# Turning the decayed RWKV-7 state with four full-array transposes instead of sixteen identity products, under a refitted schedule planner

## The chip, the cores and the metric

The kernel runs on one core of a Trainium2 chip. A core has five engines with queues of their own: PE (TensorE, the matrix products; PEld is its weight load), DVE (VectorE), ACT (ScalarE), POOL (GpSimd) and SP (SyncE, which here issues all transfers). They meet only through semaphores. The metric is the device time of one execution in microseconds. The kernel before took 717.02 us, the median of three runs (716.88 to 718.17).

## The reference, cut to what matters

```python
# attention block: B, H, S, D = 4, 8, 768, 40; float32
state = zeros(B, H, D, D)
for t in range(S):
    y[:, :, t] = einsum('bhd,bhde->bhe', r[t], state)
    Sa = einsum('bhde,bhe->bhd', state, a[t])
    state = state * w[t][:, :, None, :] - einsum('bhd,bhe->bhde', Sa, b[t])
    state = state + einsum('bhd,bhe->bhde', v[t], k[t])
# dense block on x = y as (3072 tokens, 320)
h = x @ w_in            # 320 -> 2048
g = h * sigmoid(1.702 * h)
out = g @ w_out         # 2048 -> 320
```

Everything is float32. The recurrence runs over 768 tokens for 32 pairs of batch and head, and its output feeds two dense layers.

## The kernel before

**Tiling.** The sequence is cut into 12 chunks of 64 tokens, and each chunk into two *units* (two batches each), 24 units in all: unit i is chunk i // 2, half i % 2. Within a unit the recurrence becomes products of 64x64 blocks. A 128-partition tile is used as two halves of 64, so that four 64x64 products run in the four quarters of the PE array; `mm` (L330) issues all products. The letters e, f, b, u are the bits that name a head, a batch and a half; `slot(b, u, f)` gives a block's place.

**One unit.** `decay` takes logarithms and cumulated sums of w and their exponentials (`FT`, `GT`, `G`, and `wch`, `wz` for the decay over a chunk). `prep` scales a, b and k with them and forms the score blocks `A` and `RV`. `inverse` inverts a triangular block by five doubling steps (`ps_level`), with DVE transposes and copies between them, then `ps_Q` and `ps_T`, which complete the inverse `T`. `solve` reads the old state, forms `B`, multiplies with the inverse (`ps_X`, masked into `M`), and `ps_y` gives both the unit's output and the new state `zraw`. `read_out` and `decayed` make `x`, which goes to DRAM (`x_dram`) and comes back in the order that the dense layers need (`xT_all`); both transfers are SP's.

**The state.** For each unit but the first two, the state `zraw` of unit i - 2 is decayed by `wz` on DVE, into columns 64 to 103 of the eight 104-column blocks of `zr` (L866). `state_turned` transposes it: 16 products with an identity, each a 64x64 block of which 40 columns are wanted, into both banks of a PSUM pair (`ps_zT`). A copy (L878) brings the result to `zT`, `read_state` multiplies r with it (`ps_rz`), and a copy (L889) puts that into columns 0 to 63 of `zr`. The products for `B` and the sums after `ps_y` then read `zr` whole. Each `zr` buffer is cleared once at the start (L440), since products read 64 columns at a stride of 104.

**Dense layers.** `mlp(c)` holds 160 products of 256 columns (`ps_up`) and 128 of 320 columns (`ps_down`) for each chunk. It can start when x of both units of the chunk is back from DRAM and the weights are there. The weights come in eight pieces that are put together on the chip: a transfer, a step on ACT (L478), three on DVE (L482, L486, L490), and an integer addition on POOL (L494, the "join").

**The order.** Nothing is issued as it is written. `plan.add` books a task with a rank, the engines that may run it with an estimated duration on each, and what it reads and writes. `Plan.order` then plays all engines against a clock and lets the free engine take the able task of lowest rank; so it picks the engine too, where several are named. Its constants say what an instruction fetch, a transfer, a semaphore and a slow PE clock cost. `refined` then tries random changes of the ranks of tasks that start in the first 140 us, keeps those with an earlier planned end, and the tasks are issued in the order that results. A changed constant or seed can thus change each engine's order from the first instruction on. PSUM is four pairs of banks, given out by the planner; queues of each engine are in order.

Of the kernel before, what the change touches and what calls it, by code (L numbers as in the profile page):

```python
# [18 lines left out]
FP32 = mybir.dt.float32  # L19
# [4 lines left out]
ACT = mybir.ActivationFunctionType  # L24
# [35 lines left out]
class Plan:  # L60
# [3 lines left out]


    OPENING = 140000.0
    BLOCK, FETCH, AHEAD = 256, 3528.0, 300.0
    BESIDE, LARGE, BESIDE_LARGE = 0.35, 1e6, 0.63
    COLD, WINDOW, SHARE = 2.0, 2600.0, 0.45
    SWITCH = 1290.0  # L70
    MARGIN, STEADY = 0, 1e12
    DELAY = {"PE": 300.0, "DVE": 60.0, "ACT": 60.0, "POOL": 150.0, "SP": 800.0}

    BEGIN = {"PE": 0.0, "ACT": 3300.0, "DVE": 5500.0, "POOL": 10000.0, "SP": 800.0}
    LATENCY, RATE, SPREAD = 2010.0, 417.0, 1.3

    def __init__(self, slots, pairs):
        self.slots, self.pairs = slots, pairs
# [201 lines left out]
def rwkv7_gelu_quick(ctx: ExitStack, tc: tile.TileContext, time_d, v_d, w_d, wc_d, ak_d, b_d, rv_d, w_in, w_out, out):  # L280
    nc = tc.nc
    H, D, S = 8, 40, out.shape[0] // 4
    DM = H * D
# [10 lines left out]
    EARLY = 4  # L294
    BY_PE = 4
    PLAIN = 4
    ROUNDS, WINDOW, SHARE = 4, 5000.0, 1.0
    TRIES, SEED = 300, 1
    RANKS = [14, 16, 20, 24, 35, 37, 39, 41]
    HALF = [slice(0, 64), slice(64, 128)]  # L300
    BITS = (0, 1)
    QUARTERS = [(0, 0), (1, 1), (0, 1), (1, 0)]
# [3 lines left out]
    work = ctx.enter_context(tc.tile_pool(name="work", bufs=1))  # L306
    dram = ctx.enter_context(tc.tile_pool(name="dram", bufs=1, space=bass.MemoryType.DRAM))
    banks = ctx.enter_context(tc.tile_pool(name="banks", bufs=1, space=bass.MemoryType.PSUM))

    plan = Plan(dict(logw=3, wc=3, G=1, wch=3, wz=2, time=2, ak=2, b=2, rv=2, FT=3, GT=1, kh=2, bh=2, zr=2, rz=2,  # L310
                     A=1, B=1, RV=2, E0=2, W0=2, P21=2, PT=2, W=2, E=2, ES=2, EX=2, T=2, Tc=1, QT=1, zraw=2, zT=1, M=2, x=1, xT=3, g=4, ob=1), 4)
    tiles, psums, drams = {}, {}, {}

    def single(name, shape):
        return const.tile(shape, FP32, tag=name, name=name)

    def buf(name, n, shape, dt=FP32):

        if (name, n) not in tiles:
            s = n % plan.slots[name]  # L320
            tiles[name, n] = work.tile(shape, dt, tag=f"{name}{s}", name=name)
        return tiles[name, n]

    def psum(t, name):
        if t.pair not in psums:
            psums[t.pair] = banks.tile([128, 2, 512], FP32, tag=f"pair{t.bank}", name=name)
        return psums[t.pair]

    def mm(o, lhsT, rhs, start):
        nc.tensor.matmul(o, lhsT, rhs, start=start, stop=True, skip_group_check=True)  # L330
# [5 lines left out]
    def pe(*sets):  # L336

        return {"PE": sum(n * 2 * max(58.0, cols / 1.2 + 3) for n, cols in sets), "instr": sum(16 * n for n, _ in sets)}

    def dve(n):  # L340
        return {"DVE": 170.0 + 1.03 * n}
# [4 lines left out]
    def any2(n):  # L346
        return {**act(n), **dve(n)}

    def copy(e):
        return nc.scalar.copy if e == "ACT" else nc.vector.tensor_copy  # L350

    def of(e):
        return nc.gpsimd if e == "POOL" else nc.vector


    def several(name, shape):
        return [single(f"{name}{i}", shape) for i in range(plan.slots[name])]
# [4 lines left out]

    nc.scalar.preload_act_table_set("natural_log_exp_and_others")

    full = work.tile([128, 128], FP32, tag="g0", name="full")
    make_identity(nc, full)
    padded(nc.vector, ak_t[0])
    ident = single("ident", [128, 64])
# [62 lines left out]
    def preset(engine, *places):  # L431
        for t in places:
            copy(engine)(t, one32.unsqueeze(1).to_broadcast([128, 8, 32]))
# [2 lines left out]
    for t in P21_t + Tc_t:  # L436
        nc.gpsimd.memset(t[:, 8 * 32:], 0.0)
    zr_t = several("zr", [128, 8 * 104 + 24])
    for n, t in enumerate(zr_t):
        plan.add(25 + n, {"POOL": 820.0, "DVE": 950.0, "sbuf": True}, lambda t, n=n: of(t.engine).memset(zr_t[n], 0.0), writes=[("clear", n)])  # L440
    W_t, E_t, ES_t = several("W", [128, 8, 64]), several("E", [128, 8, 32]), several("ES", [128, 8, 32])
    EX_t, T_t, QT_t = several("EX", [128, 8, 2, 32]), several("T", [128, 8, 2, 32]), several("QT", [128, 8, 32])

# [98 lines left out]
    wz_of = lambda i: buf("wz", i, [128, 8])  # L542

    def slot(b, u, f):
        return 4 * u + 2 * b + f
# [89 lines left out]
    B_of, zr_of = lambda i: buf("B", i, [128, 8, 104]), lambda i: at(zr_t, i)  # L635
    both = lambda i: zr_of(i)[:, :8 * 104].rearrange("p (j n) -> p j n", n=104)
    zraw_of = lambda i: buf("zraw", i, [128, 8, D])
# [3 lines left out]
    zT_of = lambda i: zT_t[i % plan.slots["zT"]]  # L641
# [50 lines left out]
    def inverse(i):  # L692
# [10 lines left out]
        PT = at(PT_t, i).rearrange("p (j t) -> p j t", t=96)  # L703
        if i < PLAIN:
            plan.add(R - 3, {"ACT": 400.0}, lambda t: preset(t.engine, PT[:, :, 64:]), room=T("PT"), writes=T("preset"))
        elif i < PLAIN + 2:
            plan.add(R - 3, {"ACT": 800.0, "DVE": 900.0}, lambda t: preset(t.engine, at(E0_t, i), at(W0_t, i)[:, :, 32:]), room=T("PT"),
                     writes=T("preset"))

        def score_N(t):  # L710

            ps = psum(t, "ps_N")
            for f, u in product(BITS, BITS):
                for e, b in QUARTERS:
                    o, j = (2 * f + u) * 64, slot(b, u, f)
                    mm(ps[HALF[b], e, o:o + 64], ahT()[HALF[e], j], b_of(i)[HALF[e], j], o == 0)
        plan.add(R, pe((4, 64)), score_N, reads=T("ahT", "bhT") + (T("preset") if i < PLAIN + 2 else []), uses=T("ak", "b"), room=T("E0", "P21"), pair=("N", i))
        for n in BITS if i >= PLAIN else ():
            plan.add(R, dve(256), lambda t, n=n: nc.vector.copy_predicated(  # L719
# [4 lines left out]
                 writes=T("P21"), pair=("N", i))  # L724
        if i >= PLAIN:
            plan.add(R, {"DVE": 430.0, "POOL": 750.0, "sbuf": True}, lambda t: of(t.engine).tensor_sub(  # L726
                at(W0_t, i)[:, :, :32], two32.unsqueeze(1).to_broadcast([128, 8, 32]), at(E0_t, i)), reads=T("E0"), writes=T("W0"))

        def turned(rank, source, reads, n, dst, writes):

            plan.add(rank, dve(256), lambda t: nc.vector.transpose(ES(n), source(t)), writes=[key("ES", n, 6)], **reads)  # L731

            def spread(t):
                if t.engine == "ACT":
                    for h in BITS:
                        nc.scalar.activation(dst[:, :, h], ES(n), ACT.Copy, scale=quads[:, h, :1])  # L736
                else:
                    of(t.engine).tensor_mul(dst, ES(n).unsqueeze(2).to_broadcast([128, 8, 2, 32]),
                                            quads.unsqueeze(1).to_broadcast([128, 8, 2, 32]))
            plan.add(rank, {"POOL": 1390.0, "DVE": 700.0, "ACT": 910.0, "sbuf": True}, spread, reads=[key("ES", n, 6)], writes=writes)  # L740

        if i >= PLAIN:
            turned(R, lambda t: at(E0_t, i), dict(reads=T("E0")), 0, EX(0), [key("EX", 0, 5)])
# [115 lines left out]
    def solve(i):  # L859
        c, p = divmod(i, 2)  # L860
        R = 20 * (i // 2) + 5 * (i % 2)
        T = lambda *names: [(n, i) for n in names]
        ahT = lambda: ak_of(i)[:, 0]

        if c > 0:
            plan.add(R, {"DVE": 490.0, "sbuf": True}, lambda t: nc.vector.tensor_mul(  # L866
                both(i)[:, :, 64:], zraw_of(i - 2), wz_of(i).unsqueeze(2).to_broadcast([128, 8, D])),
                     reads=[("zraw", i - 2), ("wz", i)], writes=T("zr"))

            def state_turned(t):  # L870

                ps = psum(t, "ps_zT")
                for u, b in product(BITS, BITS):
                    for e, f in QUARTERS:
                        o, k = (2 * u + b) * D, slot(b, u, f) * 104 + 64
                        mm(ps[HALF[f], e, o:o + D], zr_of(i)[HALF[e], k:k + 64], ident[HALF[e], :D], o == 0)
            plan.add(R, pe((4, 40)), state_turned, reads=T("zr") + ([("clear", p)] if c == 1 else []), room=T("zT"), pair=("zT", i))
            plan.add(R, any2(320), lambda t: copy(t.engine)(  # L878
                zT_of(i)[:, :DM].rearrange("p (r n) -> p r n", r=2), psum(t, "")[:, :, :160]), writes=T("zT"), pair=("zT", i))

            def read_state(t):

                ps, rT = psum(t, "ps_rz"), rv_of(i)[:, 0]
                for u, b in product(BITS, BITS):
                    for f, e in QUARTERS:
                        o, at = (2 * u + b) * 64, (4 * e + 2 * u + b) * D
                        mm(ps[HALF[e], f, o:o + 64], zT_of(i)[HALF[f], at:at + 64], rT[HALF[f], 4 * u + 2 * e + b], o == 0)
            plan.add(R, pe((4, 64)), read_state, reads=T("rv", "zT"), pair=("rz", i))
            plan.add(R, any2(512), lambda t: copy(t.engine)(  # L889
                both(i)[:, :, :64].rearrange("p (j f) t -> p f j t", f=2), psum(t, "")[:, :, :256].rearrange("p f (j t) -> p f j t", t=64)),  # L890
                     reads=T("zT"), writes=T("rz"), pair=("rz", i))
# [41 lines left out]
        def read(t):  # L933

            ps = psum(t, "ps_y")
            for b, f in product(BITS, BITS):
                o = (2 * b + f) * 104
                for m, w in ((RV_of(i), kh_of(i)), (M_of(i), bh_of(i))):
# [6 lines left out]
                 pair=("y", i))  # L945
# [107 lines left out]
    for i in range(NU):  # L1053
        decay(i)
        if i + 3 < NU:
            load_w(i + 3)
        if i + 2 < NU:
            logarithm(i + 2)
        if i >= 2:
            load(i)  # L1060
        prep(i)
        inverse(i)
        solve(i)
        if i % 2:
            mlp(i // 2)
# [89 lines left out]
```

## Time and profile before

| | us |
|---|---|
| median of three runs | 717.02 |
| profiled execution, whole | 715.64 |
| its span, first to last instruction | 713.9 |
| PE busy in the span | 673.0 |
| of it ps_up and ps_down, busy | 251.7 and 243.0 |
| DVE, ACT, POOL busy | 423.8, 347.7, 204.6 |
| start of the first ps_up | 79.23 |

A group's busy time is the time in which at least one of its instructions runs. PE's records overlap, since products are pipelined, so that its groups add up to more than 673.0. "issue" in a list of waits is time in which an engine waited for nothing that the profile shows. The steps of the state's turning, in the list of groups (line, engine, operation, tiles, count, busy time, mean ns of one, idle time of the engine before them and what ended it):

```profile
L330 PE MATMUL ps_zT<-ident,zr 64*64 64x40 f32 x704 | 15.1, 223 | 0.7 <-DVE E L782 0.7
L866 DVE TENSOR_TENSOR zr<-zraw,wz 128x320 f32<-128x320 f32 x22 | 17.4, 792 | 0.6
L878 ACT COPY zT<-ps_zT 128x320 f32<-128x320 f32 x16 | 6.8, 426 | 14.7 <-PE ps_zT L330 14.6
L440 DVE MEMSET zr<- 128x856 f32 x2 | 1.5, 772 | 0.3
```

### The profile page before, as it was taken

What the parts mean: (1) busy time and instruction counts of PE and PEld (TensorE: products, weight loads), DVE (VectorE), ACT (ScalarE), POOL (GpSimd) and SP (SyncE); (2) the same over time, 40 slices, a digit from 0 to 9 for tenths busy, and PEclk for the clock granted to TensorE, in tenths of its full rate; (3) what the DMA queues carried; (4) which work ended last, traced back from release to release, by engine and by line L of the source; (5) the groups of instructions that cost most, each with busy time, mean ns of one, the idle gap of its engine ahead of it and who ended that gap; (6) DMA issues with size and microseconds to landing.
All of it is one profiled execution on the core that took longest, in us unless ns stands there. A gap on an engine that the chain in (4) does not pass through costs nothing.

```text
span 713.9 us, 43522 instructions
## 1 busy us (share of the span) xinstructions
PE 673.0 (94%) x20256; PEld 562.4 (79%) x20256; DVE 423.8 (59%) x747; ACT 347.7 (49%) x683; POOL 204.6 (29%) x260
## 2 busy tenths in 40 slices
PE   4667899999999999999999999999999999999997
PEld 4566779887888788788888998779978788877563
DVE  6689777756766576577474775666675656421000
ACT  4465636656365465454555565256445535342020
POOL 5367244442431321331342233220341320200000
PEclk9879999999999999999999999999999999999999
DMA  7955351431441341341432241251341230111000
GB/s 244 394 193 181 111 168 47 139 99 44 129 121 32 113 137 32 111 139 42 120 121 86 72 124 50 83 147 33 107 115 32 81 96 5 41 49 31 20 3 19
DMA packets 31860, 69.81 MB, mean 98 GB/s; under 512 B 5056, under 2 KB 14272, under 8 KB 30656
## 3 DMA queue, kind: packets, MB, share of 16 engines
q1 hardware_dynamic: 31680, 67.03, 30.5%
q8 instruction: 159, 2.61, 1.5%
q14 instruction: 21, 0.17, 0.1%
HBM read 59.15 MB, written 7.86 MB: 94 GB/s over the span
## 4 chain that ended last, share of the span: by engine, by line
PE 88%; DVE 5%; issue 3%; DMA 2%; ACT 1%; SPq 0%; ACTq 0%; DVEq 0%
PE ps_down L330 29%; PE ps_up L330 28%; PE ps_level L330 9%; PE ps_y L330 4%; PE ps_B L330 4%; PE ps_X L330 2%; PE ps_T L330 1%; PE ps_Q L330 1%; PE ps_rz L330 1%; PE ps_A L330 1%; PE ps_RV L330 1%; PE ps_N L330 1%; PE ps_zT L330 1%; PE ps_cum L330 1%; DMA rv<-in_rv 1%
## 5 line engine op out<-in xcount | busy, mean ns | idle before, releaser
L330 PE MATMUL ps_up<-xT_all,w_sb 64*64 64x256 f32 x3840 | 251.7, 378 | 1.8 <-issue 1.7
L330 PE MATMUL ps_down<-w_sb,g 64*64 64x320 f32 x3072 | 243.0, 431 | 0.8 <-issue 0.6
L330 PEld LDWEIGHTS ps_up<-xT_all,w_sb 64*64 64x64 f32 x3840 | 157.5, 133 | 27.1 <-issue 2.7
L330 PEld LDWEIGHTS ps_down<-w_sb,g 64*64 64x64 f32 x3072 | 131.1, 133 | 45.4 <-issue 2.4
L736 ACT ACTIVATE EX<-ES,quads 128x256 f32<-128x256 f32 x124 | 56.2, 501 | 56.8 <-DVE ES L731 56.4
L1008 ACT ACTIVATE g<-ps_up 128x1024 f32<-128x1024 f32 x48 | 49.1, 1024 | 39.6 <-PE ps_up L330 39.4
L330 PEld LDWEIGHTS ps_level<-W,EX 64*64 64x64 f32 x2560 | 57.5, 134 | 8.3 <-ACT zT L878 1.0
L780 ACT COPY W<-ps_level 128x512 f32<-128x512 f32 x55 | 32.2, 586 | 55.3 <-PE ps_level L330 54.7
L657 POOL TENSOR_TENSOR kh<-time,G 128x320 f32<-128x320 f32 x23 | 20.9, 910 | 131.9 <-PE ps_y L330 70.7
L330 PE MATMUL ps_level<-W,EX 64*64 64x64 f32 (+1 forms) x2560 | 55.7, 218 | 0.9 <-ACT zT L878 0.6
L782 DVE TENSOR_TENSOR E<-two,ps_level 128x256 f32<-128x256 f32 x80 | 33.2, 415 | 39.1 <-ACT W L780 38.7
L1034 DVE TENSOR_TENSOR ob<-ob,ps_down 128x320 f32<-128x320 f32 x24 | 11.6, 482 | 59.6 <-ACT ob L1032 58.7
L726 POOL TENSOR_TENSOR PT<-two,PT 128x256 f32<-128x256 f32 x18 | 13.1, 728 | 109.8 <-DVE PT L719 105.1
L330 PE MATMUL ps_level<-PT,EX 64*64 64x64 f32 (+2 forms) x1280 | 37.5, 250 | 5.0 <-issue 4.0
L330 PEld LDWEIGHTS ps_level<-PT,EX 64*64 64x64 f32 x1280 | 35.4, 152 | 7.9 <-issue 4.9
L973 POOL TENSOR_TENSOR x<-zr,FT 128x128 f32<-128x128 f32 x80 | 40.9, 539 | 0.0
L731 DVE STREAM_TRANSPOSE ES<-E 128x256 f32<-128x256 f32 x80 | 35.6, 444 | 3.9
L911 ACT COPY B<-ps_B 128x416 f32<-128x416 f32 x38 | 19.1, 504 | 37.2 <-PE ps_B L330 36.9
L330 PE MATMUL ps_y<-RV,kh 64*64 64x104 f32 x768 | 35.7, 251 | 1.4 <-DVE M L927 1.4
L330 PE MATMUL ps_y<-M,bh 64*64 64x104 f32 x768 | 35.6, 249 | 1.2 <-issue 1.2
L649 POOL TENSOR_TENSOR ak<-ak,FT 128x512 f32<-128x512 f32 x16 | 21.5, 1345 | 50.0 <-DMA ak<-in_ak 31.0
L1032 ACT COPY ob<-ps_down 128x320 f32<-128x320 f32 x22 | 9.4, 425 | 53.1 <-PE ps_down L330 53.0
(136 smaller groups left out, 1168.1 us busy)
## 6 DMA issues: line engine op xcount, KB each, us to landing
time<-in_time SPq DMA_DIRECT2D x24, 320.0 KB
ak<-in_ak SPq DMA_DIRECT2D x48, 160.0 KB
rv<-in_rv SPq DMA_DIRECT2D x48, 160.0 KB
xT_all<-x_dram SPq DMA_DIRECT2D x48, 160.0 KB
wc<-in_wc SPq DMA_DIRECT2D x20, 264.0 KB
logw<-in_w SPq DMA_DIRECT2D x24, 160.0 KB
RV<-in_v SPq DMA_DIRECT2D x24, 160.0 KB
b<-in_b SPq DMA_DIRECT2D x48, 80.0 KB
```

The source lines that it names most:

```text
L330: nc.tensor.matmul(o, lhsT, rhs, start=start, stop=True, skip_group_check=True)
L649: plan.add(R, {"DVE": 690.0, "POOL": 1270.0, "sbuf": True}, lambda t: of(t.engine).tensor_mul(ahT(), ahT(), FT_of(i)), reads=T("ak", "FT") ...
L657: plan.add(R + 4, {"POOL": 870.0, "DVE": 490.0, "sbuf": True}, lambda t, n=n, dst=dst: of(t.engine).tensor_mul(dst(i)[:, :, :D], by_head(t ...
L726: plan.add(R, {"DVE": 430.0, "POOL": 750.0, "sbuf": True}, lambda t: of(t.engine).tensor_sub(at(W0_t, i)[:, :, :32], two32.unsqueeze(1).to ...
L731: plan.add(rank, dve(256), lambda t: nc.vector.transpose(ES(n), source(t)), writes=[key("ES", n, 6)], **reads)
L736: nc.scalar.activation(dst[:, :, h], ES(n), ACT.Copy, scale=quads[:, h, :1])
L780: plan.add(rank, any2(512), lambda t: copy(t.engine)(tiles_of(W(n + 1)), blocks(psum(t, ""), 64)), writes=[key("W", n + 1, 5)], pair=pair)
L782: plan.add(rank, dve(256), lambda t: nc.vector.tensor_sub(tiles_of(E(n + 1)), every(two32, [128, 2, 4, 32]), blocks(psum(t, ""), 64)[:, :, ...
L911: plan.add(R, any2(416), lambda t: copy(t.engine)(dst(), psum(t, "")[:, :, :208]), writes=[("Bv", i)] if x and c > 0 else T("B"), pair=(na ...
L973: of(t.engine).tensor_mul(x[:, b ^ u, b], both(i)[:, at, :64], FT_of(i)[:, at])
L1008: plan.add(-45, {"ACT": 1030.0, "table": "gelu"}, lambda t: nc.scalar.activation(g_of(c * NQ + q).rearrange("p m r n -> p r m n"), psum(t, ...
L1034: plan.add(-45, dve(320), lambda t: nc.vector.tensor_add(ob_of(serial), ob_of(serial), psum(t, "")[:, 1, :DM]), reads=[("ob", serial)], wr ...
```

## The change

The decayed state is written to a tile of its own, `zc`, whose blocks are 64 columns wide, two side by side making 128. A copy, on ACT, DVE or POOL as the planner chooses, brings it to `zr`. The turning becomes four transposes of 128x128 into one bank of the pair, with `full`, the 128x128 identity that was built before in a borrowed buffer and now has one of its own. The read-out to `zT` picks the 320 wanted columns of 512. The two clears of `zr` go; the unused columns of `zc` are cleared instead. There is one `zc` for both units of a chunk, so the next unit's decay waits for the copy and the turning of the one before.

The planner books 400 ns and 8 instructions for the four transposes, where it booked four sets of four products and 64 instructions. Its other constants change too, as do the number of tries and the seed of the search.

```diff
-    BLOCK, FETCH, AHEAD = 256, 3528.0, 300.0
-    BESIDE, LARGE, BESIDE_LARGE = 0.35, 1e6, 0.63
-    COLD, WINDOW, SHARE = 2.0, 2600.0, 0.45
+    BLOCK, FETCH, AHEAD = 256, 3460.0, 300.0
+    BESIDE, LARGE, BESIDE_LARGE = 0.43, 1e6, 0.55
+    COLD, WINDOW, SHARE = 1.9, 3400.0, 0.5
...
-    LATENCY, RATE, SPREAD = 2010.0, 417.0, 1.3
+    LATENCY, RATE, SPREAD = 1830.0, 370.0, 1.3
...
+    TURN = 400.0
-    TRIES, SEED = 300, 1
+    TRIES, SEED = 350, 3
...
-    full = work.tile([128, 128], FP32, tag="g0", name="full")
+    full = single("full", [128, 128])
...
-    for n, t in enumerate(zr_t):
-        plan.add(25 + n, {"POOL": 820.0, "DVE": 950.0, "sbuf": True}, lambda t, n=n: of(t.engine).memset(zr_t[n], 0.0), writes=[("clear", n)])
+    zc = single("zc", [128, 8, 64])
+    plan.add(24, {"POOL": 550.0, "DVE": 300.0, "sbuf": True}, lambda t: of(t.engine).memset(zc[:, :, D:], 0.0), writes=[("clear", 2)])
...
             plan.add(R, {"DVE": 490.0, "sbuf": True}, lambda t: nc.vector.tensor_mul(
-                both(i)[:, :, 64:], zraw_of(i - 2), wz_of(i).unsqueeze(2).to_broadcast([128, 8, D])),
-                     reads=[("zraw", i - 2), ("wz", i)], writes=T("zr"))
+                zc[:, :, :D], zraw_of(i - 2), wz_of(i).unsqueeze(2).to_broadcast([128, 8, D])),
+                     reads=[("zraw", i - 2), ("wz", i)], writes=T("zc"))
+            plan.add(R, {"ACT": 460.0, "DVE": 400.0, "POOL": 750.0, "sbuf": True}, lambda t: (nc.scalar.copy if t.engine == "ACT" else of(t.engine).tensor_copy)(
+                both(i)[:, :, 64:], zc[:, :, :D]), reads=T("zc"), writes=T("zr"))
...
                 for u, b in product(BITS, BITS):
-                    for e, f in QUARTERS:
-                        o, k = (2 * u + b) * D, slot(b, u, f) * 104 + 64
-                        mm(ps[HALF[f], e, o:o + D], zr_of(i)[HALF[e], k:k + 64], ident[HALF[e], :D], o == 0)
-            plan.add(R, pe((4, 40)), state_turned, reads=T("zr") + ([("clear", p)] if c == 1 else []), room=T("zT"), pair=("zT", i))
+                    o, j = (2 * u + b) * 128, slot(b, u, 0)
+                    nc.tensor.transpose(ps[:, 0, o:o + 128], zc[:, j:j + 2].rearrange("p j n -> p (j n)"), full)
+            plan.add(R, {"PE": TURN, "instr": 8}, state_turned, reads=T("zc") + ([("clear", 2)] if i == 2 else []), room=T("zT"), pair=("zT", i))
             plan.add(R, any2(320), lambda t: copy(t.engine)(
-                zT_of(i)[:, :DM].rearrange("p (r n) -> p r n", r=2), psum(t, "")[:, :, :160]), writes=T("zT"), pair=("zT", i))
+                zT_of(i)[:, :DM].rearrange("p (r j n) -> p r j n", r=2, n=D),
+                psum(t, "")[:, 0].rearrange("p (j r n) -> p r j n", r=2, n=64)[:, :, :, :D]), writes=T("zT"), pair=("zT", i))
```

More of the change, by code (lines that the diff above doesn't have):

```diff
@@ L308, in rwkv7_gelu_quick @@
     banks = ctx.enter_context(tc.tile_pool(name="banks", bufs=1, space=bass.MemoryType.PSUM))
-    plan = Plan(dict(logw=3, wc=3, G=1, wch=3, wz=2, time=2, ak=2, b=2, rv=2, FT=3, GT=1, kh=2, bh=2, zr=2, rz=2,
+    plan = Plan(dict(logw=3, wc=3, G=1, wch=3, wz=2, time=2, ak=2, b=2, rv=2, FT=3, GT=1, zc=1, kh=2, bh=2, zr=2, rz=2,
                      A=1, B=1, RV=2, E0=2, W0=2, P21=2, PT=2, W=2, E=2, ES=2, EX=2, T=2, Tc=1, QT=1, zraw=2, zT=1, M=2, x=1, xT=3, g=4, ob=1), 4)
```

## The prediction

> **What bounds the kernel now.** I read the page's busy shares and its forty slices first, then the busy time by stretches, then the list of waits, then the timeline of the stretch where the waits are.
>
> ```profile
> PE 673.0 (94%) x20256; PEld 562.4 (79%) x20256; DVE 423.8 (59%) x747; ACT 347.7 (49%) x683; POOL 204.6 (29%) x260
> PE   4667899999999999999999999999999999999997
> PEclk9879999999999999999999999999999999999999
> ```
>
> TensorE is busy in all but the first slices, and its granted clock is low in the same ones. The stretches give sizes; the columns are the stretch, its length, the busy time of PE, PEld, DVE, ACT and POOL, the granted clock and the DMA.
>
> ```profile
> 0.00:20.00 20.00, 9.43 (x303) 8.83 (x307) 14.52 (x22) 8.91 (x28) 12.77 (x48) 1.00 0.78 262
> 20.00:40.00 20.00, 12.73 (x374) 11.27 (x365) 11.45 (x20) 11.52 (x20) 5.13 (x5) 0.75 0.92 355
> 40.00:60.00 20.00, 15.34 (x592) 14.39 (x595) 18.44 (x22) 12.17 (x31) 14.12 (x12) 0.82 0.49 157
> 60.00:80.00 20.00, 13.87 (x507) 12.34 (x503) 16.40 (x21) 10.52 (x21) 10.77 (x10) 0.91 0.66 210
> 80.00:700.00 620.00, 612.54 (x18380) 510.72 (x18376) 362.06 (x664) 303.77 (x583) 161.80 (x189) 1.00 0.28 80
> ```
>
> PE idles 28.6 us before 80 us (80 less 9.43, 12.73, 15.34 and 13.87) and 7.5 us in the 620 us after it. So three things can change the time: PE work removed or added, at full price from 80 us on; the idle opening; and what little idle time there is later. An edit on DVE, ACT or POOL counts only in the opening.
>
> The opening ends when the first product of the dense layers (ps_up) starts, since these fill every gap from then on. The timeline shows what it waits for (columns: start, length, engine, line, operation):
>
> ```profile
> 58.74 1.95 DVE L486 TENSOR_SCALAR w_sb<-w_sb 128x1280 int32<-128x1280 int32 x1
> 60.61 1.01 DVE L927 TENSOR_TENSOR M<-ps_X,later 128x832 f32<-128x832 f32 x1
> 62.66 2.96 POOL L494 TENSOR_TENSOR w_sb<-w_sb,extra 128x1280 int32<-128x1280 int32 x1 [0.85 <-DVE extra L490]
> 63.72 0.59 ACT L965 COPY zr<-ps_y 128x512 f32<-128x512 f32 x1
> 65.59 2.94 POOL L973 TENSOR_TENSOR x<-zr,FT 128x128 f32<-128x128 f32 x4
> 68.56 0.67 SPq L983 DMA_DIRECT2D x_dram<-x  x2
> 74.83 1.09 SPq L987 DMA_DIRECT2D xT_all<-x_dram  x2
> 79.23 1.60 PE L330 MATMUL ps_up<-xT_all,w_sb 64*64 64x256 f32 x24
> ```
>
> Read from the bottom: the dense layers start at 79.23 when x of unit 1 is back from DRAM; x was made on POOL from 65.59, having stood behind a weight join (62.66 to 65.62) although its input was there at 64.31; and unit 1's chain before it lost time behind weight work on DVE (L486 before M).
>
> **Prices of PE work** come from the chain of waits, where work stands alone (start, length, group, number of records):
>
> ```profile
> 623.41 0.46 PE ps_zT L330 x30
> 651.01 1.43 PE ps_y L330 x64
> 655.24 4.32 PE ps_up L330 x80
> 694.05 15.12 PE ps_down L330 x224
> ```
>
> Sixteen products leave 32 records, so each float32 product is two passes, and four 64x64 products run side by side in a pass. One pass of 320 columns takes 15.12/56 = 0.27 us, one of 256 takes 4.32/20 = 0.216: 0.84 ns a column. Sixteen narrow products, such as today's turning, cost 0.45 us.
>
> **The turning of the state.** Removed: 22 x 0.45 = 9.9 us of PE. Added: 22 x 4 transposes, each of 128 columns over the whole array. The trace has none. In one pass each costs 128 x 0.84 = 0.108 us, four 0.43 us, and the edit is worth 22 x 0.02 = 0.4 us gained. With two passes, as every product in the trace has, four cost 0.86 us and the edit loses 22 x 0.41 = 9.0 us. If a transpose were as cheap as the narrowest record here (0.46/32 = 0.014 us, eight of them 0.11 us) it would gain 7.5 us. I take one pass, since the new code books 8 instructions for the four turnings (a load and a product each) where it books 64 for the sixteen products that it replaces (two of each); both ends stay in the range. The 56 fewer instructions a unit have little to save: the longest idle PE time named "issue" after 80 us is 1.7 us in one place, and all others are 1.2 us or less.
>
> [...]
>
> **What the other engines do for it.** The product that decays the state now writes zc, as large as before. A copy zc to zr is added, 22 times: 17 on ACT, 4 on DVE, 1 on POOL by the new order. On ACT a copy of 320 columns is 0.425 us (L878), 7.2 us in all, but the new order has 27 activation-table loads where there were 33, 6 x 1.283 = 7.7 us less. Cover: ACT is busy 304 of the 620 us, and the B products that read zr also wait for ps_rz, a copy, two PE steps and an ACT step later. If that cover went, the 0.43 us would stand on a chain that PE fills with dense work anyway. The read-out from PSUM moves the same 320 columns: nothing. The two clears of zr (0.77 us each on DVE at 5.9 to 7.6) become a smaller one, which gains nothing: DVE waits for the ak transfer until 8.57.
>
> **The new order**, which the fitted constants and the other search bring, is the larger part. I compared the two built orders on each queue.
> - *Opening.* Between the results (ps_y) of units 0 and 1, PE now issues four steps (ps_Q, ps_T, ps_X, ps_RV), where there were eleven (unit 2's A, RV, N, both cumulated sums, the turning, a level and ps_rz besides). Today it takes from 50.14 to 61.67, 11.5 us. The new stretch: y 1.9, Q 0.67, QT 0.48, ps_T 0.62, T 0.44, X 0.94, M 1.01, and about 0.2 us for each of five hand-overs: 7.1 us, 4.4 us less. DVE holds three weight steps between M of unit 0 and T of unit 1, 2.4 us at 0.8 us each; they lie beside y and Q, and cost up to 2 us if two of them run at 1.95 us like L486 above. On POOL the join ahead of x of unit 1 comes earlier, and one zc copy (about 0.75 us) stands there instead, ready about when x is. So x starts 4.4 to 5.7 us earlier; I take 5. The way from x to ps_up has the same transfers: 13.6 us. The dense layers then start near 74.2. But two levels (0.88 us each), a last level (0.68) and a turning (0.45), 2.9 us of work, now come after that point. Gain: 5.0 - 2.9 = 2.1 us. Bounds: 5 if x gains all of its 5.7 us and the weight steps never bite; a loss of 2 if these do and unit 0's own chain comes later too.
> - *Stock of dense work.* A chunk's dense work is 160 + 128 products, 17.3 us each kind, 34.5 us. What may be issued before the next chunk's x exists is 34.5 us for each chunk read out; the order says how much of it is left when the second unit of the next chunk reads out. Units counted from 1: 7.5, 5.4, 8.5 and 9.6 us were left at units 4, 6, 8 and 10, now 12.9, 16.1, 12.8 and 16.1. The way from a read-out to ps_up is 16 us above, so the new stock covers more of it. All that it can save is in the 7.5 us of idle PE after 80 us, part of which is instruction supply: I take 1 us, between a gain of 4 and a loss of 1.
> - *Queues.* SP issues the same 245 entries; logw of unit 2 moves ahead of ak of unit 0, and time behind it, which leaves ak with fewer bytes ahead. POOL gets 6 more spreads (1.28 us), 7 more of the small wz and a copy, and is busy 29%.
>
> Sum: 0.4 + 2.1 + 1.0 = 3.5 us. The profiled execution has 713.9 us of span and 1.7 us around it, 715.6; its span becomes 710.4. The median shown is 1.4 us above that execution: 717.0 - 3.5 = **713.5 us**.
>
> **The rivals.**
> 1. *The transposes take the array twice.* Place: 22 times on PE, most of them after 80 us, where PE has no slack. For it: every float32 product in the trace has two records, and a full-array product has no neighbours to run beside. Against it: the instruction count in the code. Price +9.0, the order's 3.1 still gained: 717.0 + 5.9 = 723. It decides the sign from 0.45 + 3.1/22 = 0.59 us a unit on.
> 2. *The order gains nothing.* The weight steps on DVE take the place of the join as the wait, so ps_up starts at 79 with 2.9 us less done, and a better stock gives that back: 716 to 718, shown as 717. For it: L486 takes 1.95 to 3.45 us when POOL works beside it. Against it: DVE has those steps beside work that must run anyway.
> 3. *Both parts near their good ends.* Opening 5, stock 2, cheap transposes 3: 717.0 - 10 = 707. For it: the opening's idle time is 28.6 us, so there is room; against it: the clock there is granted by stretches and a new order needn't meet better ones.
>
> **Chances.** Forecast 0.50 (710 to 715.5), rival 1 0.18, rival 2 0.16, rival 3 0.16. About 0.2%, 1.4 us, is what a measurement tells from no change. Faster: all of the forecast and of rival 3, 0.66; same: most of rival 2, 0.13; slower: rival 1 and the rest, 0.21. The range runs from 706.5, just below rival 3, to 721.5, which leaves out the worse half of rival 1 and a few that go past rival 3.
>
> **What would show it.** ps_zT: four records a unit and not eight, and 0.43 us from its start to the next group. First ps_up near 74, x of unit 1 on POOL near 60.5. PE idle after 80 us at 6 to 7 us. I am wrong if ps_zT takes over 0.6 us a unit, if ps_up starts after 77, or if some chunk's x comes late and ps_up or ps_down waits for a DMA in mid-run.

## The result, and the profile after

The changed kernel is slower: 724.26 us (median of four runs, 723.07 to 730.56) against 717.60 for the kernel before on the same chip (four runs, 716.88 to 718.66). The ratio is 1.014, 95% interval 1.0095 to 1.0185. Two repeats on other chips gave 1.0102 (1.0063 to 1.0140) and 1.0133 (1.0088 to 1.0177). The forecast was 713.5. The profiled execution has a span of 721.4 us, 7.5 more than before.

The busy shares of the engines and two rows of the page's forty slices, as they were shown of before (PEclk is the TensorE clock that was granted, in tenths of full speed):

```profile
PE 678.1 (94%) x19640; PEld 524.4 (73%) x19640; DVE 434.0 (60%) x755; ACT 339.4 (47%) x674; POOL 215.9 (30%) x274
PE   5577898999999999999999999999999999999997
PEclk9769899999999999999999999999999999999999
```

PE has 616 products fewer, and DVE and POOL are busy some 10 and 11 us longer, though DVE has only 8 instructions more. The busy time by stretches (stretch, length, PE, PEld, DVE, ACT, POOL, granted clock, DMA):

```profile
0.00:20.00 20.00, 10.11 (x346) 9.48 (x347) 14.88 (x24) 9.11 (x29) 13.30 (x48) 1.00 0.78 250
20.00:40.00 20.00, 12.63 (x354) 11.54 (x357) 9.27 (x14) 8.22 (x20) 0.20 (x1) 0.70 0.92 359
40.00:60.00 20.00, 14.38 (x511) 12.50 (x503) 18.69 (x18) 10.87 (x21) 15.29 (x10) 0.79 0.47 153
60.00:80.00 20.00, 12.62 (x408) 10.53 (x411) 18.12 (x21) 9.06 (x23) 11.58 (x12) 0.89 0.47 142
80.00:700.00 620.00, 611.79 (x17789) 471.01 (x17792) 372.12 (x680) 300.30 (x581) 175.56 (x204) 1.00 0.29 83
```

PE's idle time is 30.3 us before 80 us (28.6 before the change) and 8.2 after it (7.5). That is 2.4 us of the 7.5. Busy shares do not show PE busy at a low clock, nor work that was not yet done when the dense layers began. So I made a ledger from the trace: each record of a product, ps_zT aside, counts a quarter of 0.84 ns a column (the prediction's price) and at least 14.5 ns; added up in order of start this is 632 us in both kernels. *Lost* is the time so far less the work so far:

| lost, us | until first ps_up (its start) | from there to 80 us of work (131 to 142 us) | from there to the last product | sum |
|---|---|---|---|---|
| before, first trace | 47.9 (79.23) | 3.0 | 25.4 | 76.3 |
| before, second trace (r_before) | 47.4 (78.71) | 3.6 | 26.4 | 77.4 |
| after, first trace | 44.8 (73.72) | 15.0 | 23.9 | 83.7 |
| after, second (r_after) | 44.8 (73.68) | 17.7 | 24.3 | 86.8 |
| after, third (r_after2) | 43.0 (71.90) | 15.5 | 27.3 | 85.8 |

Up to the first ps_up the change gains 3 to 5 us. In the next 60 us it loses 11 to 15, some 13. Later the two are alike. The timeline of after has the places (start, length, engine, line, operation; in brackets the idle time before and what ended it):

```profile
58.03 3.20 POOL L495 TENSOR_TENSOR w_sb<-w_sb 128x1280 int32<-128x1280 int32 x1
58.34 3.23 DVE L867 TENSOR_TENSOR zc<-zraw,wz 128x320 f32<-128x320 f32 x1
61.64 0.45 POOL L870 COPY zr<-zc 128x320 f32<-128x320 f32 x1 [0.41 <-DVE zc L867]
62.05 1.70 POOL L976 TENSOR_TENSOR x<-zr,FT 128x128 f32<-128x128 f32 x4
62.23 1.11 PE L878 MATMUL ps_zT<-full,zc 128*128 128x128 f32 x4 [2.49 <-DVE A L669]
64.95 0.72 SPq L986 DMA_DIRECT2D x_dram<-x  x2
67.86 1.09 SPq L990 DMA_DIRECT2D xT_all<-x_dram  x2
73.72 2.77 PE L331 MATMUL ps_up<-xT_all,w_sb 64*64 64x256 f32 x48
...
75.43 3.26 POOL L495 TENSOR_TENSOR w_sb<-w_sb,extra 128x1280 int32<-128x1280 int32 x1 [4.46 <-DVE w_sb L487]
75.88 3.38 DVE L565 TENSOR_TENSOR_SCAN wc<-starts,wc 128x264 f32<-128x264 f32 x1
79.19 0.68 DVE L753 STREAM_TRANSPOSE EX<-ps_level 128x512 f32<-128x512 f32 x1
79.36 0.63 ACT L609 ACTIVATE FT<-wc 128x512 f32<-128x512 f32 x1 [3.50 <-DVE wc L565]
79.93 1.56 PE L331 MATMUL ps_level<-PT,EX 64*64 64x96 f32 x32 [3.43 <-DVE EX L753]
80.62 0.41 ACT L622 ACTIVATE G<-ps_cum 128x320 f32<-128x320 f32 x1
...
107.74 3.24 POOL L495 TENSOR_TENSOR w_sb<-w_sb,extra 128x1280 int32<-128x1280 int32 x1 [4.18 <-DMA extra<-in_w_out]
108.14 3.40 DVE L565 TENSOR_TENSOR_SCAN wc<-starts,wc 128x264 f32<-128x264 f32 x1
112.44 0.43 DVE L732 STREAM_TRANSPOSE ES<-ps_level 128x256 f32<-128x256 f32 x1
112.91 0.91 ACT L737 ACTIVATE T<-ES,quads 128x256 f32<-128x256 f32 x2 [1.07 <-DVE ES L732]
113.87 0.67 PE L331 MATMUL ps_Q<-T,P 64*64 64x32 f32 x32 [2.42 <-ACT T L737]
```

Three times the same picture. A join runs on POOL; a DVE row that starts 0.3 to 0.45 us after it, and takes 0.45 us (zc, at 74.16) or 0.70 us (the other scan, at 75.26) where no join is running when it starts, ends 0.34 to 0.57 us after the join does; everything queued behind it on DVE, and then PE, waits. Such a row is called held from here on. The first case, before the dense layers, makes PE wait 2.49 us for A, whose DVE row stands behind zc. For x of unit 1, which came at 62.05 and not at the 60.5 that was forecast, it counts only 0.41 us: POOL itself was in the join until 61.23, and then had the copy to `zr` ahead of x. The second is worst: the dense products have started, but PE's queue has a ps_level next, which waits 3.43 us for EX, whose DVE row stands behind the scan. After that wait the same 32 records take 1.56 us, where they took 0.89 at 72.79 with a granted clock of 1.00, and the granted clock from 80 to 90 us is 0.70. The two repeats show both later waits again, 3.4 us for EX and 3.0 and 2.9 for ps_Q. The trace has the 3.38 us as the scan's own length, with no wait before it, where it has 0.70 for the one before: so the engines of a core do not meet only through semaphores.

The kernel before has held rows too. One after its first ps_up:

```profile
111.21 2.96 POOL L494 TENSOR_TENSOR w_sb<-w_sb,extra 128x1280 int32<-128x1280 int32 x1
111.87 2.86 DVE L649 TENSOR_TENSOR ak<-ak,FT 128x512 f32<-128x512 f32 x1
```

PE goes on with ps_Q and dense products meanwhile. Its longest wait for a DVE row between 74 and 140 us is 0.3 us in that trace and 0.9 in the second. So the two kernels differ less in the held rows than in what PE's queue has in front while they last.

The rows held here, the scans and the zc product, have both inputs in SBUF; a weight step that was held earlier (L487, 3.45 us at 50.09) has one input. What makes them wait for the join is not shown by any run. Nor do the runs show which wait costs clock. The wait of 3.43 us in the first trace is followed by a granted clock of 0.50 from 79.9 to 82 us and 0.55 from there to 86.4. In r_after the wait for ps_Q is 3.0 us, and the granted clock from 110 to 120 us is 0.66; in the first trace it is 2.42 us, and the clock behind it, from 113.8 to 120, is 1.00.

### The profile page after: what moved, and what is told of

It is laid out like the page before. It is cut to its first block, busy times and chain, and to the rows that moved or that the text cites. A ratio compares the mean times of both kernels' runs of the same rounds, so it can differ in the third digit from the quotient of the medians.

```text
span 721.4 us, 42313 instructions
## 1 busy us (share of the span) xinstructions
PE 678.1 (94%) x19640; PEld 524.4 (73%) x19640; DVE 434.0 (60%) x755; ACT 339.4 (47%) x674; POOL 215.9 (30%) x274
## 4 chain that ended last, share of the span: by engine, by line
PE 87%; DVE 6%; issue 3%; ACT 2%; DMA 1%; POOL 0%; DVEq 0%; ACTq 0%; SPq 0%
PE ps_down L331 29%; PE ps_up L331 27%; PE ps_level L331 9%; PE ps_B L331 4%; PE ps_y L331 4%; PE ps_X L331 2%; PE ps_zT L878 2%; PE ps_A L331 2%; PE ps_N L331 2%; PE ps_T L331 1%; PE ps_rz L331 1%; PE ps_RV L331 1%; PE ps_Q L331 1%; PE ps_cum L331 1%; DVE EX L753 1%
## 5 line engine op out<-in xcount | busy, mean ns | idle before, releaser
L331 PE MATMUL ps_up<-xT_all,w_sb 64*64 64x256 f32 x3840 | 242.6, 379 | 0.3 <-ACT g L1011 0.3
L331 PE MATMUL ps_down<-w_sb,g 64*64 64x320 f32 x3072 | 232.6, 431 | 0.0
L331 PEld LDWEIGHTS ps_up<-xT_all,w_sb 64*64 64x64 f32 x3840 | 136.7, 134 | 41.3 <-issue 2.4
L331 PEld LDWEIGHTS ps_down<-w_sb,g 64*64 64x64 f32 x3072 | 118.3, 133 | 56.2 <-issue 1.3
L737 ACT ACTIVATE EX<-ES,quads 128x256 f32<-128x256 f32 x116 | 52.6, 501 | 46.4 <-DVE ES L732 46.3
L331 PEld LDWEIGHTS ps_level<-W,EX 64*64 64x64 f32 x2560 | 52.5, 134 | 14.6 <-issue 2.2
L658 POOL TENSOR_TENSOR kh<-time,G 128x320 f32<-128x320 f32 x24 | 22.6, 940 | 103.4 <-issue 58.8
L331 PE MATMUL ps_level<-W,EX 64*64 64x64 f32 (+1 forms) x2560 | 52.3, 218 | 1.1 <-issue 0.9
L331 PE MATMUL ps_level<-PT,EX 64*64 64x64 f32 (+2 forms) x1280 | 36.6, 252 | 14.5 <-issue 8.2
L727 POOL TENSOR_TENSOR PT<-two,PT 128x256 f32<-128x256 f32 x17 | 12.5, 737 | 80.0 <-DVE PT L720 80.0
L930 DVE TENSOR_TENSOR M<-ps_X,later 128x832 f32<-128x832 f32 x24 | 24.4, 1018 | 16.5 <-PE ps_X L331 16.4
L739 POOL TENSOR_TENSOR EX<-ES,quads 128x512 f32<-128x512 f32 x14 | 19.5, 1390 | 37.1 <-DVE ES L732 37.1
```

Of the source, the lines that this page charges most:

```text
L658: plan.add(R + 4, {"POOL": 870.0, "DVE": 490.0, "sbuf": True}, lambda t, n=n, dst=dst: of(t.engine).tensor_mul(dst(i)[:, :, :D], by_head(t ...
L930: plan.add(R + 1, dve(832), lambda t: nc.vector.tensor_tensor(M_of(i).rearrange("p (j b) n -> p b j n", b=2), psum(t, "")[:, :, :416].rear ...
```

## The experiments

Letters in the expectations: theory A, the transposes are dear; theory C, DVE rows held by joins cost the time; other letters are explained where they stand. Ratios are to the kernel before, run beside it on the same chip. On these chips the kernel before itself went from about 708 to 720 us, so only ratios are compared, and single traces only by where their time goes. The kernel as changed stands at 1.0102 to 1.0140.

**Is it the transposes?** Three runs. *e1_products_same_order* has the changed kernel's order on every engine, with the sixteen products reading `zc`:

```diff
-                    nc.tensor.transpose(ps[:, 0, o:o + 128], zc[:, j:j + 2].rearrange("p j n -> p (j n)"), full)
+                    for e, f in QUARTERS:
+                        o = (2 * u + b) * D
+                        mm(ps[HALF[f], e, o:o + D], zc[HALF[e], slot(b, u, f)], ident[HALF[e], :D], o == 0)
```

> The changed kernel with its order on every engine kept, and only the turning put back: 16 products with the identity from zc in place of the four transposes. Theory A (the transposes are dear): in the changed kernel's trace 0.59 us from the first transpose to the next group, and some 0.1 us more of pause before it, against 0.44 us; 22 units give 3 to 6 us, so 718 to 721 us where the changed kernel has 724. Theory B (the new order alone is slower): no more than 1 us from the changed kernel.

Measured 727.66, ratio 1.0198 (1.0162 to 1.0234): slower still. PE's waits named issue add up to 14.2 us against 11.1; what they stand for is not shown. *e13_turned_twice* issues each transpose twice:

> The changed kernel with each of the four transposes of a unit issued twice into the same place. If the turning takes the 0.59 us a unit that the trace shows and is on PE's path: 22 x 0.43 to 22 x 0.59, 9.5 to 13 us more than the changed kernel, ratio to the kernel before 1.024 to 1.032. If they overlap other PE work (the records overlap one another): below 5 us, under 1.019. If each costs its record's 272 ns in full: 22 x 1.09 = 24 us, 1.045.

Measured 733.3, ratio 1.0266 (1.0227 to 1.0305), which is 0.0126 to 0.0164 over the changed kernel, 9 to 12 us. The ps_zT group of after, then of e13 (count, busy time, mean ns of one):

```profile
L878 PE MATMUL ps_zT<-full,zc 128*128 128x128 f32 x88 | 15.4, 300 | 3.0 <-DVE A L669 2.5 <-DVE ES L732 0.5
```

```profile
L879 PE MATMUL ps_zT<-full,zc 128*128 128x128 f32 x176 | 24.6, 284 | 0.6 <-DVE A L669 0.4 <-DVE ES L732 0.2
```

88 more records add 9.2 us of busy time, 0.105 us each. From the first transpose of a unit to the next group are 0.59 us in after (20 of 22 units) and 1.02 in e13. So a transpose costs about one pass, 0.108 us in the prediction, and not two. *e7_before_transposes* keeps the order of before and turns with transposes from a `zc` that an extra DVE copy fills for each unit:

> The kernel before with its order kept on every engine, and only the turning changed: four transposes from zc in place of 16 products, zc filled by one more DVE copy (320 columns, about 0.46 us) right after the state is decayed. Theory A (transposes dear, 0.59 + 0.1 us against 0.44): 3 to 6 us above the kernel before. Theory D (transposes as such are a gain, since 56 fewer PE instructions a unit spare stalls of instruction supply; run e1 lost by going back): 1 to 4 us below the kernel before.

Measured 718.17, ratio 1.0061 (1.0028 to 1.0093), 0.6% slower with 22 copies that the real change does not have; it says little for or against A by itself. With e1 and e13, theory A falls.

**Is it the joins?** If a held row lasts to the end of a join, cutting the joins should let it end with a piece, unless DVE gets no turn between the pieces. *e2_split_joins* leaves the order and cuts each join into four; *e14_split_two* cuts it into two:

```diff
-            nc.gpsimd.tensor_tensor(out=scale(), in0=scale(), in1=word(INT32, 1), op=ALU.add)
+            for k in range(4):
+                s = slice(k * PIECE // 4, (k + 1) * PIECE // 4)
+                nc.gpsimd.tensor_tensor(out=scale()[:, s], in0=scale()[:, s], in1=word(INT32, 1)[:, s], op=ALU.add)
```

> The changed kernel with its order kept, and each weight join on POOL cut into four instructions of 320 columns. [...]

> The changed kernel with each join in two POOL instructions of 640 columns, order kept. Theory C (a VectorE row that starts during a join lasts to its end): a half takes about 0.335 + 640 x 0.0023 = 1.8 us by the rows of 1280 and 320 columns (3.27 and 1.07 us), so rows are held to at most 1.8 + 0.5 us and the time lies between the changed kernel and the quarters: ratio 1.003 to 1.010. Theory D (the split of e2 helped by chance, by shifting all later rows): no order between whole, halves and quarters; 1.010 or more is as likely.

e2 measured 716.18, ratio 1.0041 (1.0008 to 1.0074), and again, beside r_after2, 716.42, ratio 1.0009 (0.9976 to 1.0043): 9 us below the changed kernel's 725.58 on the same chip.

> The changed kernel with its order kept and the joins cut into four, on one chip with the changed kernel. Theory C: 5 to 9 us below the changed kernel, as the first such run (1.004 of the kernel before) says if chips are alike. Rival: the gain was the chip's: within 2 us of it.

e14 measured 719.31, ratio 1.0037 (1.0005 to 1.0068). The timeline of e2 at the place that is 75.43 to 79.93 above (its lines are numbered two higher):

```profile
71.30 4.71 POOL L497 TENSOR_TENSOR w_sb<-w_sb,extra 128x320 int32<-128x320 int32 x4 [2.73 <-DVE w_sb L487]
71.75 1.32 DVE L567 TENSOR_TENSOR_SCAN wc<-starts,wc 128x264 f32<-128x264 f32 x1
72.99 0.69 DVE L755 STREAM_TRANSPOSE EX<-ps_level 128x512 f32<-128x512 f32 x1
73.73 0.89 PE L331 MATMUL ps_level<-PT,EX 64*64 64x96 f32 x32 [1.17 <-DVE EX L755]
```

The scan takes 1.32 us and not 3.38, PE waits 1.17 us and not 3.43, and the granted clock from 70 to 90 us is 1.00, though POOL is busy longer in all (4 x 1.07 us for 3.27). PE's waits in 74 to 140 us, after and then e2 (total, times, longest):

```profile
PE ps_level L331 <- DVE EX L753: 3.7, 2, 3.4
PE ps_Q L331 <- ACT T L737: 2.4, 1, 2.4
PE ps_level L331 <- issue: 1.6, 1, 1.6
```

```profile
PE ps_level L331 <- DVE EX L755: 1.4, 2, 1.2
PE ps_level L331 <- issue: 1.4, 1, 1.4
PE ps_Q L331 <- ACT T L739: 1.2, 1, 1.2
```

Whole joins lose 15.0 to 17.7 us in the ledger's middle part, halves 9.9, quarters 9.2 and 9.1. With halves PE's longest waits for EX and ps_Q are 2.1 and 1.8 us, between the other two. In that part PE idles 8.1, 7.8 and 8.2 us in the three traces of the changed kernel, and 4.2 and 4.3 in the two of e2. The granted clock over it is 0.95, 0.90 and 0.95, and 1.00 with quarters; the missing 0.05 and 0.10 of 66 to 69 us are worth some 3 to 7 us at most (an estimate). So of the 6 to 9 us that quarters get back there, some 4 are waits, and by that estimate the slow clock is enough for the rest. Two things are not explained by it. Quarters also gain ahead of the dense layers: the first ps_up comes at 69.42 and 70.52 us, with 40.5 and 41.6 us lost. And they still lose some 6 us more in the middle part than the kernel before, so that e2 ends 0.1 to 0.4% above it.

In the order of before the same edit should do less:

> The kernel before with its order kept and the joins cut into four. Theory C: its own long rows beside joins (L486 3.45 us, L651 3.06, L657 1.97, L486 1.95) fall, PE's wait of 2.9 us for T at 46.7 us goes, and the first ps_up comes earlier: a gain of 2 to 5 us, 712 to 716. Rival: no turn between the pieces, within 1 us of 717.6.

Measured 714.70, ratio 1.0022 (0.9993 to 1.0050): nothing gained, so the forecast gain was a miss. In the first trace of before PE waits only 0.3 us for EX in 74 to 140 us, so there was little to gain. *e8_before_transposes_split*, e7 with split joins, gave 721.31, 1.0071 (1.0044 to 1.0097), so nothing there either.

> The same with the joins cut into four. Theory C and D together: not above the run without the cut, and 1 to 5 us below the kernel before. If cutting the joins helps the new order alone, it is within 1 us of the run without the cut.

*e6_both* has products and split joins in the order of after:

> The changed kernel's order with cut joins and with 16 products in place of the transposes. Theory A (transposes dear in themselves): 3 to 5 us below the run with cut joins alone, so at or below the kernel before. Theory D (the products pay as much in instruction supply where this order puts them): 0 to 4 us above it.

Measured 720.06, ratio 1.0048 (1.0007 to 1.0089), beside e2's 716.42 on the same chip. Against e1's 1.0198 this is the gain of the split joins a second time, with the other way of turning. With them the transposes are no worse than the products, and perhaps 3 us better; the intervals overlap.

**Which held row?** *e10_scan_later* moves the two scans of the fifth unit (75.26 and 75.88 above) two DVE rows later, behind EX. In this run that unit's FT, GT and wch are taken from logarithms that are not yet summed, so ACT does not wait for the scans.

```diff
     tasks = plan.refined(TRIES, SEED)
+    s = next(n for n, t in enumerate(tasks) if t.fn.__name__ == "sums")
+    e = [n for n, t in enumerate(tasks) if n > s and t.engine == "DVE"][2 - 1]
+    tasks.insert(e, tasks.pop(s))
```

> The changed kernel with one move on DVE alone: the two scans of the fifth unit (L564, L565), which stand before the transpose EX that PE waits 3.4 us for at 76.5 us, go behind it and behind the mask of A. Both steps read PSUM. Theory C: the long row beside the join at 75.4 us is still there, on the scan, but PE no longer waits for it; the wait of 3.4 us at 76.5 shrinks below 1 us, and the half clock that follows it at 79.5 to 86.4 us goes or gets shorter: 3 to 6 us below the changed kernel. If any DVE instruction is held by the join, EX is held in the scan's place and nothing is gained.

Measured 720.79, ratio 1.0070 (1.0041 to 1.0099), 4.8 us below the changed kernel on the same chip. It takes away ACT's wait for the scans as well as DVE's order, so it does not show which of the two counted. *e11_scan_later* does it with the exponentials moved too, so that nothing is left out:

```diff
+    late = [tasks[s]]
+    for t in tasks[s + 1:e + 1]:
+        if any(o in t.after for o in late):
+            late.append(t)
+    tasks[s:e + 1] = [t for t in tasks[s:e + 1] if t not in late] + late
```

> The changed kernel with one edit of its order: the two scans of the fifth unit, and what depends on them, stand two VectorE rows later, so that the matrix-free exponential mask of that stretch is not behind a scan that lasts to the end of a join; nothing is left out of the computation. Theory C (rows held by joins, 8.5 us lost between 80 and 140 us): the 3.43 us wait for EX at 79.9 us goes, the granted clock there stays at full, 3 to 5 us below the changed kernel (ratio to the kernel before 1.003 to 1.008), as with e10. Theory D (the new order as a whole is worse, the joins are only where it shows): within 1.5 us of the changed kernel, 1.011 to 1.014; the wait turns up later, at the exponentials that now come later.

Measured 727.18, ratio 1.0180 (1.0151 to 1.0208): theory C's figures missed, and its rival's wait came. Its timeline:

```profile
74.57 2.96 POOL L495 TENSOR_TENSOR w_sb<-w_sb,extra 128x1280 int32<-128x1280 int32 x1 [4.55 <-DVE w_sb L487]
75.04 0.72 DVE L753 STREAM_TRANSPOSE EX<-ps_level 128x512 f32<-128x512 f32 x1 [0.54 <-ACT PT L814]
76.26 1.84 DVE L564 TENSOR_TENSOR_SCAN wc<-starts,wc 128x264 f32<-128x264 f32 x1
78.02 0.68 DVE L565 TENSOR_TENSOR_SCAN wc<-starts,wc 128x264 f32<-128x264 f32 x1
78.79 0.63 ACT L609 ACTIVATE FT<-wc 128x512 f32<-128x512 f32 x1 [3.78 <-DVE wc L565]
80.05 0.41 ACT L622 ACTIVATE G<-ps_cum 128x320 f32<-128x320 f32 x1
80.52 1.56 PE L331 MATMUL ps_level<-PT,EX 64*64 64x96 f32 x32 [3.60 <-ACT G L622]
```

EX is early now, but the first scan is held all the same (1.84 us). FT waits for the scans at the head of ACT's queue, and so does G behind FT, which reads ps_cum; PE waits 3.60 us for G. In e10 nothing on ACT waited for the scans. *e12_scan_later_split* is e11 with quarters:

> e11's order with each join in four POOL instructions of 320 columns. Theory C: the split has already taken the waits away, so moving the scans adds at most 1 us: 714 to 717 by e2's ratio, 0.998 to 1.003. If holds of the scans by one quarter of a join still cost, 1 to 3 us below e2, 0.996 to 0.999, faster than both kernels.

Measured 720.31, ratio 1.0083 (1.0052 to 1.0114): 7 us below e11 on the same chip, but 3 to 5 us above e2 by the ratios. A miss for all that was expected. The wait for G is still there:

```profile
74.62 1.44 DVE L566 TENSOR_TENSOR_SCAN wc<-starts,wc 128x264 f32<-128x264 f32 x1
75.97 1.30 DVE L567 TENSOR_TENSOR_SCAN wc<-starts,wc 128x264 f32<-128x264 f32 x1
79.10 1.56 PE L331 MATMUL ps_level<-PT,EX 64*64 64x96 f32 x32 [3.82 <-ACT G L624]
```

The two scans take 0.74 and 0.60 us more than the usual 0.70, 1.3 us in all; in e11 it was 1.1. So no more than that of the 3.60 and 3.82 us is the hold; the rest comes with the later place of the scans, with ACT behind them. Here cutting the join served, and moving the row did not.

**Is it the constants and the search?** *e4_after_old_plan* is the changed kernel with the constants, tries and seed of before, *e5_before_new_plan* the kernel before with those of after. Both are new orders.

> The changed kernel with the planner's old constants, tries and seed; the transposes and zc stay, so that the order is a third one. Theory A alone: the kernel before plus 3 to 6 us, 721 to 724. Theory B (the new constants and search are at fault): 719 or less. An order is also a draw of its own, so this run says little by itself; its first ps_up, PE's idle time before and after 80 us and the price of the turning are to be read.

> The kernel before with the scheduler's constants, tries and seed of the changed kernel; 16 identity products as before. Theory C (an order found without the price of a held row can fall on the joins by chance): no set sign, 0.995 to 1.015, and the trace shows scans held for 2.4 to 3.5 us with PE behind them in 80 to 140 us where it is slow. Theory A (the transposes are at fault): not slower than before, 0.997 to 1.003.

e4: 721.47, ratio 1.0105 (1.0055 to 1.0156). e5: 719.05, ratio 1.0053 (1.0024 to 1.0082). The old constants do not bring the changed kernel back, and the new ones cost the kernel before some 0.5%; since both are new orders, constants and chance are not told apart. From the first ps_up on, held rows explain little in either. e5 has a scan held for 2.81 us at 99.14 and no wait of PE behind it. e4 is about as slow as the changed kernel, and its trace has

```profile
89.59 3.41 DVE L565 TENSOR_TENSOR_SCAN wc<-starts,wc 128x264 f32<-128x264 f32 x1
93.43 0.94 PE L331 MATMUL ps_X<-B,T 64*64 64x104 f32 x32 [1.02 <-DVE T L854]
99.58 3.39 DVE L565 TENSOR_TENSOR_SCAN wc<-starts,wc 128x264 f32<-128x264 f32 x1
```

PE waits 1.02 us behind the first scan and not at all behind the second, and loses 8.0 us in the ledger's middle part. So a new order can be 1% slow with little of it behind such rows; what slows e4, and whether split joins would help it, was not tried. The wording of e5, that the search has no price for a held row, was wrong: `Plan.order` books POOL's rows and DVE's SBUF rows one after the other (`shared = max(now, shared) + t.engines[e]`). Why it still places PE behind such rows was not tried. Last, the joins were given to the search as four steps of 320 columns:

> The changed kernel with each join as four steps of 320 columns that the search places one by one, at 1.07 us each, and the order searched anew with them. If the length of a join was what made the new order slow, this one has the split's gain too, and room between the quarters: 0.994 to 1.002, at or below the kernel before. If each new order is a new draw with a spread of about 1%, anything from 0.995 to 1.015, with waits of PE in the first 140 us at other places.

Measured 717.92, ratio 1.0012 (0.9979 to 1.0044), with 5.3 us lost in the ledger's middle part. That, e2 and e3 are within some 0.4% of the kernel before. No version beat it.

## Why the prediction was wrong

- **The turning**, +0.4 us: right in kind. One record a transpose, 0.105 us each by e13, against 0.108. From start to next group it takes 0.59 us and not 0.43: e13's four more add 0.43, so some 0.16 is the group's start and end. Sixteen products take 0.44 alone but 0.54 on average in before, so the 22 units lose about 1 us where 0.4 was booked as a gain. By e13 a transpose costs about half of a product of 128 columns, which is an estimated 0.215 us (two records at 0.84 ns a column). Its record is 272 ns long, but the four of a unit overlap (0.66 us in all at 119.00).
- **Copies and clears at nothing**: no wait for the copy to `zr` stands in the lists of PE's waits, but one copy stood on POOL ahead of x of unit 1 (0.45 us). It was not tried alone in the new order.
- **The opening up to the first ps_up**, +2.1 us: right in the number, partly by luck. It started at 73.72 (forecast 74.2), and the ledger gives 3 to 5 us. But the way there was another. A join did stand ahead of x of unit 1: it ran on POOL from 58.03 to 61.23, while x's input was there at 58.72 (the copy after ps_y, L968, 58.13 and 0.59 long). With the wait for `zc` and the copy, x was 1.5 us late. And the first ps_up did not wait for x: its row has no idle time before it, so it stood behind other products in PE's queue. In e4, where it did wait for x, the idle time is 2.24 us.
- **The step that failed** is the sentence that the opening ends with the first ps_up "since these fill every gap from then on", with its companion that the DVE steps "lie beside" and cost up to 2 us. PE's queue is in order: dense products fill a gap only where they stand in front of the waiting product, and from 76.5 to 79.9 us a ps_level stood there, with PE busy for none of the 3.4 us. And the sum priced DVE beside POOL by one weight step (L486, 1.95 us), and for weight steps alone. The trace before had the larger price on other rows: L649 above, and L651 at 63.12, whose 3.06 us end 0.55 after the join of 62.66. The new order lost some 13 us between 74 and 142 us, where the forecast had nothing; with the joins in quarters 6 to 9 of them came back. What makes the rest is open.
- **Stock of dense work**, +1 us: not to be seen. That a part of the idle time after 80 us is instruction supply was the author's estimate; the lists name it issue, 1.7 us at the longest. The last part of the ledger has 23.9, 24.3 and 27.3 us after, 25.4 and 26.4 before.
- **The rivals.** The first, dear transposes, came out near the measured time (723), but for a wrong cause: that is luck. The second had the mechanism, weight steps as the new wait, but only ahead of ps_up and with a price that left the time unchanged. What it missed was that the rows held were scans and the state product, with PE behind them after the dense layers had begun. The 3 us that the third has for cheap transposes no run shows: e13's cost 0.105 us each.
- **The signs** that the prediction named for being wrong did not come clearly: 0.59 us for most turnings, the first ps_up at 73.72, no wait of PE for a transfer in mid-run. None of them looked at PE's waits for DVE just after the first ps_up.

Split joins alone take the time from 1.0102 to 1.0140 down to 1.0009 to 1.0041, and from 1.0198 to 1.0048 with products, while they change nothing in the order of before. So in this order the length of the joins is shown to carry most of the loss. That any new order is slow for this reason is not shown, as e4 says.

## What to carry to other kernels

Where two engines hold each other up, look for rows of one kind with very different lengths, find what runs beside the long ones, and price every row that may be held there by the end of that neighbour (here 3.38 us for 0.70), along each queue behind it. Cutting the long instruction costs that engine time (4.3 us for 3.3) and can still pay when the other side has TensorE behind it, as e2 did (9 us beside r_after2). Moving the held row can make a new wait, as e11 and e12 did (3.60 and 3.82 us). And before a gap is called filled, check which instruction stands first in the in-order queue.

## What the hardware showed that I had not expected

- In after, three held DVE rows ran on past the join's end for 0.11 to 0.14 us less than such a row takes unheld: 0.34 us for 0.45 (zc), 0.57 for 0.68 (scan L565) and 0.68 for 0.82 (weight step L487, 50.09 to 53.54 beside a join that ended at 52.86). A scan that had begun 0.17 us before the join (75.26) took its usual 0.70.
- Not every row is held. During the join from 97.78 to 101.26 in after, a DVE transpose (98.46), two masked copies and a row with an input in PSUM took their usual 0.45 to 0.72 us; only the next, L727 with both inputs in SBUF (100.32), was held, 1.23 us to 0.28 past the join's end.
- Transposes of 128x128 in float32 have records of 272 ns in after, but 88 more of them in e13 added 0.105 us each.
- One kernel on one chip spread over 10 us (before, 20 runs, 710.04 to 720.24). On three chips the first ps_up of the changed kernel came at 71.90 to 73.72.
